# A two-layer transformer kernel: filler reordered, layer 2 begun early, softmax sums regathered by DMA

## The chip, the cores and the metric

One core of one Trainium2 chip. The metric is the device time of one execution in microseconds; lower is better. The time before is the median of three runs.

## The reference, cut to what matters

```python
x = A_x                                   # (1, 2048, 512) bf16
x = x + _A_ref(_layernorm(x), A_wqkv, A_wo)
x = x + _B_ref(_layernorm(x), B_w1, B_w2)
x = x + _A_ref(_layernorm(x), A_wqkv, A_wo)
x = x + _B_ref(_layernorm(x), B_w1, B_w2)
```

`_A_ref` is attention with 32 heads of 16 (softmax of q k / 4 over all 2048 keys, no mask, then the projection by `wo`); `_B_ref` is `relu(x @ w1) @ w2` with 1792 hidden columns. The normalization has neither gain nor bias, and both layers share their weights.

## The kernel before, in words

The 2048 rows are cut into 4 chunks of 512 (j), each of 4 row tiles of 128. Heads are handled in 8 units per chunk (t), 4 heads to a unit; two units (t = 2T and 2T + 1) share one 128-column stripe T of Q and K. There are 16 row blocks of keys (kb), 128 rows each. A unit is 16 row blocks x 4 heads = 64 blocks, and the main loop (`attention`, L411) takes 3 blocks per slot, so a unit is 21.3 slots, a chunk 170.7 and the kernel 1366.

In a slot TensorE computes three score blocks (L441) into one of two PSUM tiles `ps_s` of three banks, ScalarE takes the exponential of all three in one instruction (L448), and TensorE multiplies an earlier slot's exponentials by V (L389) into the one bank `ps_o`. V carries a column of ones, so the softmax sums come out as one row per head beside the head's 16 rows of output. At a unit's end VectorE copies `ps_o` (L366), spreads the sums by a shuffle (L369), takes reciprocals in four pieces (L372) and multiplies (L375), one of these per slot from `dve_q`.

All other matrix work is filler: after its attention part, each slot runs pieces of two matmuls from the queues `urgent` and `work`, in order and without looking whether the operands are there (`next_piece`, `run_some`); filler has one PSUM bank, `ps_f`. `urgent` holds the Q projection of the next unit. `work` holds, once a chunk's last unit is done, the rest of that chunk (`rest_of_chunk`, L337): 4 output projections of 8 matmuls, a layer normalization, 14 groups of 4 matmuls for the hidden layer, 4 groups of 14 for the second dense layer and, in layer 1, the next layer's normalization, K and V of that chunk. The evacuation of a group is issued right behind its last matmul. A normalization (`ln_groups`, `ln_stats`) issues statistics, the inverse root by four rounds of Newton and the apply on VectorE, and the transposes on TensorE in the same slot.

What a score or V block needs is forced out first (`run_until`). At the start that is K and V of each chunk in turn, as the first unit comes to them. At the end of each layer nothing is left to overlap with: the queues are run empty (L469 to L473) with all seven banks of `ps_s` and `ps_f` in rotation (`wide`). Layer 2's attention starts only behind that.

Q and the output projection use weights padded with zeros, `wq_pad` and `wo_pad`, made at the start by GpSimd and by 32 small DMAs, so that a unit's heads lie 32 rows apart.

## Time and profile before

| | |
|---|---|
| median of three runs | 2257.32 us (2256.94 to 2257.48) |
| the profiled execution, its own time | 2257.28 us |
| its span | 2255.5 us |
| TensorE busy, ScalarE busy | 1837.2 us, 1855.8 us |
| VectorE busy, GpSimd busy | 697.0 us, 12.6 us |
| mean granted TensorE clock | 0.723 of full |

The span runs from the first to the last instruction; the execution's own time is 1.8 us longer. Busy shares are means over the whole span, and the ends and the border between the layers are part of it. TensorE's clock is granted at one of two levels, so a mean of 0.723 is a mixture of stretches.

### The profile page before, as it was taken

What the parts mean: (1) busy time and instruction counts of PE and PEld (TensorE: products, weight loads), DVE (VectorE), ACT (ScalarE), POOL (GpSimd) and SP (SyncE); (2) the same over time, 40 slices, a digit from 0 to 9 for tenths busy, and PEclk for the clock granted to TensorE, in tenths of its full rate; (3) what the DMA queues carried; (4) which work ended last, traced back from release to release, by engine and by line L of the source; (5) the groups of instructions that cost most, each with busy time, mean ns of one, the idle gap of its engine ahead of it and who ended that gap; (6) DMA issues with size and microseconds to landing.
All of it is one profiled execution on the core that took longest, in us unless ns stands there. A gap on an engine that the chain in (4) does not pass through costs nothing.

```text
span 2255.5 us, 23128 instructions
## 1 busy us (share of the span) xinstructions
PE 1837.2 (81%) x10112; PEld 511.4 (23%) x10112; DVE 697.0 (31%) x1312; ACT 1855.8 (82%) x1367; POOL 12.6 (1%) x58
## 2 busy tenths in 40 slices
PE   4578887988878787988767888879887988878886
PEld 1122222222222222222222222222222222222222
DVE  5431124432253324332342122243114322142223
ACT  1279997989989898989505999989997999989970
POOL 2000000000000000000000000000000000000000
PEclk8775557986689757987576555689557975789558
DMA  4000000000000000000000000000000000000000
GB/s 140 0 1 1 1 0 1 1 1 1 1 1 1 1 1 1 1 1 1 1 0 1 1 1 1 1 1 10 1 1 1 3 8 1 1 1 10 1 1 10
DMA packets 9653, 11.44 MB, mean 5 GB/s; under 512 B 1104, under 2 KB 9040, under 8 KB 9552
## 3 DMA queue, kind: packets, MB, share of 16 engines
q1 hardware_dynamic: 8496, 8.92, 1.2%
q8 instruction: 79, 1.29, 0.2%
q10 hardware_dynamic: 1056, 1.05, 0.1%
q14 instruction: 22, 0.18, 0.0%
HBM read 7.86 MB, written 2.10 MB: 4 GB/s over the span
## 4 chain that ended last, share of the span: by engine, by line
ACT 62%; PE 25%; DVE 11%; issue 1%; POOL 0%; SPq 0%; DMA 0%; ACTq 0%; POOLq 0%; DVEq 0%
ACT e L448 62%; PE ps_f L263 8%; PE ps_s L441 6%; PE ps_o L389 5%; PE ps_s L263 4%; DVE stats L191 2%; DVE u L366 1%; PE ps_f L237 1%; DVE ht L319 1%; DVE r L372 1%; DVE vaug L291 1%; DVE xn L230 1%; DVE ktp L272 1%; DVE q L304 1%; DVE mv L192 0%
## 5 line engine op out<-in xcount | busy, mean ns | idle before, releaser
L448 ACT ACTIVATE e<-ps_s 128x1536 bf16<-128x1536 f32 (+1 forms) x1366 | 1854.5, 1551 | 298.6 <-PE ps_s L441 295.2
L441 PE MATMUL ps_s<-q,ktp 32*128 32x512 bf16 x4096 | 697.2, 497 | 168.7 <-ACT e L448 150.3
L389 PE MATMUL ps_o<-e,vaug 128*32 128x512 bf16 x4096 | 719.9, 506 | 33.9 <-DVE u L366 33.0
L441 PEld LDWEIGHTS <-ktp 32*128 32x128 bf16 x4096 | 215.8, 95 | 762.8 <-issue 744.4
L389 PEld LDWEIGHTS <-vaug 128*32 128x32 bf16 x4096 | 143.7, 97 | 492.9 <-issue 492.9
L372 DVE RECIPROCAL r<-r 128x128 f32<-128x128 f32 x256 | 221.9, 916 | 1.2
L304 DVE CAST q<-ps_f 128x512 bf16<-128x512 f32 x62 | 42.5, 685 | 501.3 <-PE ps_f L263 501.3
L366 DVE COPY u<-ps_o 128x512 f32<-128x512 f32 x64 | 44.2, 691 | 465.6 <-PE ps_o L389 465.0
L263 PE MATMUL ps_f<-xn2T,w 128*128 128x512 bf16 x352 | 110.8, 400 | 9.1 <-DVE q L304 0.8
L237 PE MATMUL ps_f<-ident,xn 128*128 128x128 bf16 x200 | 30.4, 307 | 103.1 <-DVE xn L230 103.1
L319 DVE TENSOR_SCALAR ht<-ps_f 128x512 bf16<-128x512 f32 x88 | 60.9, 692 | 148.1 <-PE ps_f L263 148.1
L263 PE MATMUL ps_f<-w,ht 128*128 128x512 bf16 x350 | 104.5, 383 | 0.8
L263 PE MATMUL ps_f<-xnT,wq_pad 128*128 128x512 bf16 x248 | 100.9, 499 | 5.1 <-DVE x L331 1.6
L263 PE MATMUL ps_f<-wo_pad,ot 128*128 128x512 bf16 x208 | 69.2, 422 | 4.1 <-DVE ot L375 2.6
L237 PEld LDWEIGHTS <-xn 128*128 128x128 bf16 x256 | 22.0, 130 | 174.5 <-DVE xn L230 174.5
L263 PEld LDWEIGHTS <-w 128*128 128x128 bf16 x448 | 37.7, 102 | 83.9 <-issue 70.5
L313 DVE TENSOR_TENSOR x<-x,ps_f 128x512 bf16<-128x512 bf16 x26 | 17.8, 685 | 113.7 <-PE ps_f L263 113.7
L237 PE MATMUL ps_s<-ident,xn 128*128 128x128 bf16 x56 | 8.5, 307 | 46.9 <-DVE xn L230 46.9
L369 DVE STREAM_SHUFFLE r<-u 128x512 f32<-128x512 f32 x64 | 46.2, 722 | 0.0
L331 DVE TENSOR_TENSOR x<-x,ps_f 128x512 bf16<-128x512 bf16 x25 | 17.1, 686 | 91.7 <-PE ps_f L263 91.7
L263 PEld LDWEIGHTS <-ht 128*128 128x128 bf16 x448 | 31.0, 97 | 60.5 <-issue 47.1
L375 DVE TENSOR_TENSOR ot<-u,r 128x512 bf16<-128x512 f32 x64 | 44.1, 689 | 1.6
(46 smaller groups left out, 459.7 us busy)
## 6 DMA issues: line engine op xcount, KB each, us to landing
w<-in_B_w_dram SPq DMA_DIRECT2D x2, 1792.0 KB, 9.7
x<-in_A_x_dram SPq DMA_DIRECT2D x16, 128.0 KB, 3.7
out_dram<-x SPq DMA_DIRECT2D x16, 128.0 KB, 1.7
wqkv<-in_A_wqkv_dram ACTq DMA_DIRECT2D x2, 512.0 KB, 5.3
wqkv<-in_A_wqkv_dram SPq DMA_DIRECT2D x1, 512.0 KB, 6.6
wo_pad<-in_A_wo_dram SPq DMA_DIRECT2D x32, 16.0 KB, 1.7
```

The lines of the kernel that those rows point to most:

```text
L191: nc.vector.bn_stats(out=st[:], in_=x_t[j * TPC + i][:])
L237: nc.tensor.transpose(pt[:, c * P : (c + 1) * P], xn[:, c * P : (c + 1) * P], ident[:])
L263: nc.tensor.matmul(b, lhsT, rhs, start=(i == 0), stop=(i == n - 1))
L304: nc.vector.tensor_copy(out=qbuf[n % 3][:], in_=b)
L319: nc.vector.tensor_scalar(out=ht[ft][:], in0=b, scalar1=0.0, scalar2=None, op0=ALU.max)
L366: nc.vector.tensor_copy(out=u[:], in_=ps_o[:])
L369: nc.vector.stream_shuffle(out=r[:], in_=u[:], mask=[lane] * 32)
L372: nc.vector.reciprocal(out=r[:, a : a + P], in_=r[:, a : a + P])
L375: nc.vector.tensor_mul(out=ot[t][:], in0=u[:], in1=r[:])
L389: nc.tensor.matmul(ps_o[32 * g : 32 * g + 32, :], vaug[l][kb][:, 4 * T + g, 2 * e : 2 * e + 32], slot["e"][:, w, :], start=(kb == 0), stop ...
L441: nc.tensor.matmul(b[:, w, :], kt[32 * g : 32 * g + 32, kc : kc + P], qbuf[n % 3][32 * g : 32 * g + 32, :], start=True, stop=True, tile_po ...
L448: ex = nc.scalar.activation(out=e[:, :m, :], in_=b[:, :m, :], func=ACTF.Exp, scale=SCALE)
```

## The change

- **Order of filler.** Each group carries the names of what it needs. A key is marked when its producer is issued (`mark`, some with a lag in slots), and a group is picked only if all its keys were marked in an earlier slot (`ready`, `pick`); other groups may overtake. Evacuations are queued in `evac` and issued behind the next slot's exponential. The parts of a normalization and of the softmax division are items of `dve_q` with costs, issued up to 900 ns a slot. `run_until` still forces (`force`) what a block needs. A slot runs at least one piece if one is ready.
- **Start.** Layer 1's four normalizations, K of the first pair and all of V are computed ahead of the first score, their PSUM evacuated by ScalarE (`nc.scalar.copy`). The other K groups become filler. The Newton rounds are three, not four.
- **Layer 2 begun early.** The first three pairs of layer 2's first chunk run on row blocks 0 to 11 and store their sums in `acc`; then the same three pairs run on blocks 12 to 15, and `acc` is added. K and V of chunk 4 are needed only by the second part.
- **Softmax sums.** Instead of the shuffle and four reciprocals, a DMA gathers the four rows of sums to 128 partitions x 16, VectorE takes one reciprocal, a DMA writes it back and a third spreads each row to 32 partitions. The very last unit keeps the shuffle, its reciprocal and multiply in quarters.
- **One Q projection per pair.** Q of a stripe is projected once and evacuated twice, each time multiplied by a 0/1 mask per row. The multiply at a unit's end applies the same mask, and `wo` is loaded unpadded by one DMA.

```diff
+    mask = [sb([P, 1], FP32, f"mask{e}") for e in range(2)]
     wqkv = sb([P, NDC, 3 * D], BF16, "wqkv")
-    wq_pad = [sb([P, NDC, P], BF16, f"wq_pad{t}") for t in range(NT)]
-    wo_pad = [sb([P, D], BF16, f"wo_pad{t}") for t in range(NT)]
+    wo = sb([P, NDC, D], BF16, "wo")
...
+    acc = [sb([P, QS], FP32, f"acc{t}") for t in range(NACC)]
     ebuf = [sb([P, W, QS], BF16, f"e{n}") for n in range(NE)]
-    qbuf = [sb([P, QS], BF16, f"q{n}") for n in range(3)]
+    qbuf = [[sb([P, QS], BF16, f"q{n}_{e}") for e in range(2)] for n in range(2)]
...
+    cbuf = [sb([P, QS // 32], FP32, f"c{n}") for n in range(2)]
...
+    warm = sb([P, 1], FP32, "warm")
...
-    nc.scalar.dma_start(out=wqkv[:, :, 0:D], in_=wq_src[:, :, 0:D])
-    nc.sync.dma_start(out=wqkv[:, :, D : 2 * D], in_=wq_src[:, :, D : 2 * D])
+    nc.scalar.dma_start(out=wqkv[:, :, D : 2 * D], in_=wq_src[:, :, D : 2 * D])
     nc.scalar.dma_start(out=wqkv[:, :, 2 * D : 3 * D], in_=wq_src[:, :, 2 * D : 3 * D])
     for tt in range(4, NTT):
         nc.sync.dma_start(out=x_t[tt][:], in_=x_flat[tt * P : (tt + 1) * P, :])
-
+    nc.scalar.dma_start(out=wqkv[:, :, 0:D], in_=wq_src[:, :, 0:D])
+    nc.sync.dma_start(out=wo[:], in_=A_wo[:, :].rearrange("(c p) f -> p c f", p=P))
+    nc.sync.dma_start(out=w1[:], in_=B_w1[:, :].rearrange("(c p) f -> p c f", p=P))
+    nc.sync.dma_start(out=w2[:], in_=B_w2[:, :].rearrange("(c p) f -> p c f", p=P))
+
+    nc.gpsimd.memset(warm[:], 0.0)
+    nc.scalar.activation(out=warm[:], in_=warm[:], func=ACTF.Exp)
...
-    for t in range(NT):
-        nc.gpsimd.memset(wq_pad[t][:], 0.0)
...
-    for t in range(NT):
-        T, e = divmod(t, 2)
-        nc.gpsimd.tensor_copy(
-            out=wq_pad[t][:].rearrange("p c (g e d) -> p c g e d", g=4, e=2)[:, :, :, e, :],
-            in_=wqkv[:, :, T * P : (T + 1) * P].rearrange(
-                "p c (g e d) -> p c g e d", g=4, e=2
-            )[:, :, :, e, :],
-        )
-    for t in range(NT):
-        nc.gpsimd.memset(wo_pad[t][:], 0.0)
-        T, e = divmod(t, 2)
...
-            nc.sync.dma_start(out=wo_pad[t][r0 : r0 + DH, :], in_=A_wo[DH * h : DH * h + DH, :])
...
+    def mark(key, lag=0):
+        made[key] = slot[0] + lag
...
+    def ready(deps):
+        return all(k in made and (wide[0] or made[k] < slot[0]) for k in deps)
...
+    evac = deque()
+    urgent = []
+    work = []
+    dve_q = []
...
+    def pick(test):
+        for q in (urgent, work):
+            for g in q:
+                if test(g["deps"]):
+                    q.remove(g)
+                    cur.extend(g["pieces"])
+                    return True
+        return False
+
+    def run_pe(budget):
         while budget > 0:
-            piece = next_piece()
-            if piece is None:
-                return
-            piece[1]()
-            budget -= piece[0]
+            if not cur:
+                if evac or not pick(ready):
+                    return
+            c, fn = cur.popleft()
+            fn()
+            budget -= c
...
+    def run_dve(budget):
+        i = 0
+        while i < len(dve_q) and budget > 0:
+            c, deps, fn = dve_q[i]
+            if ready(deps):
+                dve_q.pop(i)
+                fn()
+                budget -= c
...
+    def force():
+
+        if evac:
+            run_evac()
+            return True
+        if cur or pick(emitted):
+            cur.popleft()[1]()
+            return True
+        for i, (c, deps, fn) in enumerate(dve_q):
+            if emitted(deps):
+                dve_q.pop(i)
+                fn()
+                return True
+        return False
...
-        for _ in range(4):
...
-                    fin(b)
+                    evac.append(lambda: fin(b))
...
+        for _ in range(3):
...
+    def ln_rows(tag, j, i):
+
+        if tag not in ln_seq:
+            ln_seq.append(tag)
+        prev = ln_seq[ln_seq.index(tag) - 1]
+        dve_q.append((750, [], lambda: ln_stats(tag, j, i)))
+        if i == TPC - 1:
+            dve_q.append((2400, [], lambda: ln_rstd(tag)))
+            for k in range(TPC):
+                dve_q.append((420, [("xT", prev, k)], lambda k=k: ln_apply(tag, j, k)))
...
+    def ln_groups(tag, dst, war):
+        groups = []
+        for i in range(TPC):
+
+            def piece(i=i):
+                pt = ln_transpose(tag, i)
+
+                def fin():
+                    nc.vector.tensor_copy(out=dst[:, :, i * P : (i + 1) * P], in_=pt)
+                    mark(("xnT", tag, i))
+
+                evac.append(fin)
+
+            groups.append({"pieces": [(1.3, piece)], "deps": [("xn", tag, i)] + war})
...
+    def q_group(run, n, l, j, T):
+        def fin(b):
+            for e in range(2):
+                nc.vector.tensor_scalar(
+                    out=qbuf[n % 2][e][:], in0=b, scalar1=mask[e][:, 0:1], scalar2=None,
+                    op0=ALU.mult,
+                )
+            mark(("q", n))
 
         return mm_group(
-            [(wqkv[:, c, D + T * P : D + (T + 1) * P], xnT[j][:, c, :]) for c in range(NDC)], fin
-        )
...
-    def q_group(n, t, j):
-        def fin(b):
-            nc.vector.tensor_copy(out=qbuf[n % 3][:], in_=b)
-            done.add(("q", n))
-
-        return mm_group([(wq_pad[t][:, c, :], xnT[j][:, c, :]) for c in range(NDC)], fin)
...
+    def o_group(l, j, i):
         tt = j * TPC + i
 
         def fin(b):
             nc.vector.tensor_add(out=x_t[tt][:], in0=x_t[tt][:], in1=b)
-
-        return mm_group([(ot[t][:, i * P : (i + 1) * P], wo_pad[t][:]) for t in range(NT)], fin)
-
-    def h_group(ft):
+            mark(("o", l, j, i))
+            ln_rows(("ln2", l, j), j, i)
+
+        return mm_group(
+            [(ot[t][:, i * P : (i + 1) * P], wo[:, t // 2, :]) for t in range(NT)], fin,
+            [("ot", l, j, t, i) for t in range(NT)],
+        )
...
+            if wide[0] and ft % 2:
+                nc.scalar.activation(out=ht[ft][:], in_=b, func=ACTF.Relu)
+            else:
...
+            else:
+                ln_rows(("ln1", 1, j), j, i)
...
+            gs += ln_groups(("ln1", 1, j), xnT[j], [])
+            gs.append(k_group(1, 0, j))
+            gs += [v_group(1, kb) for kb in range(j * TPC, (j + 1) * TPC)]
+            gs += [k_group(1, T, j) for T in range(1, 4)]
...
+    segs = []
...
+    for j in range(NQS):
+        for T in range(4):
+            add_run(0, j, T, range(NKB), False, False)
+    early = range(NKB - TPC)
+    late = range(NKB - TPC, NKB)
+    for T in range(NACC // 2):
+        add_run(1, 0, T, early, False, True)
+    for T in range(NACC // 2):
+        add_run(1, 0, T, late, True, False)
+    for T in range(NACC // 2, 4):
+        add_run(1, 0, T, range(NKB), False, False)
+    for j in range(1, NQS):
+        for T in range(4):
+            add_run(1, j, T, range(NKB), False, False)
...
+        if sg["store"]:
+            nc.vector.tensor_copy(out=acc[t][:], in_=ps_o[:])
+            return
...
+        if sg["load"]:
+            nc.vector.tensor_add(out=u[:], in0=acc[t][:], in1=ps_o[:])
+        else:
+            nc.vector.tensor_copy(out=u[:], in_=ps_o[:])
...
+        def mul(a, w):
+            nc.vector.scalar_tensor_tensor(
+                out=ot[t][:, a : a + w], in0=u[:, a : a + w], scalar=mask[e][:, 0:1],
+                in1=r[:, a : a + w], op0=ALU.mult, op1=ALU.mult,
+            )
...
+        if last:
+            nc.vector.stream_shuffle(out=r[:], in_=u[:], mask=[lane] * 32)
+            for a in range(0, QS, P):
+                nc.vector.reciprocal(out=r[:, a : a + P], in_=r[:, a : a + P])
+                mul(a, P)
+        else:
+            sums = u[lane : P : 32, :]
+            nc.sync.dma_start(out=c[:], in_=sums)
+            mark(("c", n), 2)
+
+            def recip():
+                nc.vector.reciprocal(out=c[:], in_=c[:])
+                nc.sync.dma_start(out=sums, in_=c[:])
+                nc.sync.dma_start(
+                    out=r[:],
+                    in_=bass.AP(
+                        tensor=sums.tensor, offset=sums.offset,
+                        ap=[list(sums.ap[0]), [0, 32], [1, QS]],
+                    ),
+                )
+                mark(("r", n), 4)
+
+            dve_q.append((250, [("c", n)], recip))
+            dve_q.append((700, [("r", n)] + war, lambda: mul(0, QS)))
+        if t == NT - 1:
+            work.extend(rest_of_chunk(l, j))
...
+            if kb == sg["kbs"][-1] and g == 3:
+                finish_segment(sg, sg is segs[-1])
...
+    for j in range(NQS):
+        tag = ("ln1", 0, j)
+        for i in range(TPC):
+            ln_stats(tag, j, i)
+        ln_rstd(tag)
...
+        for i in range(TPC):
+            ln_apply(tag, j, i)
+            pt = ln_transpose(tag, i)
+            nc.scalar.copy(out=xnT[j][:, :, i * P : (i + 1) * P], in_=pt)
+            mark(("xnT", tag, i))
...
+        k_fin(0, 0, j, plain(k_mms(0, j)))
+        if j == 0:
+            urgent.append(q_group(None, 0, 0, 0, 0))
+            run_all()
+        for kb in range(j * TPC, (j + 1) * TPC):
+            nc.scalar.copy(out=v_out(0, kb), in_=v_in(plain(v_mms(kb))))
+            mark(("v", 0, kb))
+    for T in range(1, 4):
+        work.extend(k_group(0, T, j) for j in range(NQS))
...
+    blocks = deque((sg, kb, g) for sg in segs for kb in sg["kbs"] for g in range(4))
+    per_chunk = NT * NKB * 4 / W
+    wide[0] = False
...
+        for sg, kb, g in now:
+            if sg["n"] not in seen:
+                seen.add(sg["n"])
+                n = sg["n"] + 1
+                if n < len(runs):
+                    urgent.append(q_group(None, n, *runs[n]))
+            run_until(("q", sg["n"]))
+            run_until(("k", sg["l"], sg["T"], kb // TPC))
...
+        run_evac()
+        for sg, kb, g in now:
+            run_until(("v", sg["l"], kb))
...
-                dve_q.popleft()()
...
-            rest = len(blocks) / W % per_chunk
...
-            run_some(max(todo / max(rest - 6.0, 4.0), 0.01) if todo else 0)
-        drain_pv(0)
-        wide[0] = True
-        while dve_q:
-            dve_q.popleft()()
-        run_all()
...
+        pend.append({"e": eb, "blocks": deque(x + (w,) for w, x in enumerate(now))})
+        rest = len(blocks) / W % per_chunk
+        todo = left()
+        if todo:
+            run_pe(max(todo / max(rest - 12.0, 6.0), 1.0))
+        run_dve(900)
+    while pend:
+        emit_pv()
+    wide[0] = True
+    run_all()
...
```

## Rows read from the trace of the kernel before

**Rows 1.** The page: its parts 1 (busy us, share, instructions) and 4 (chain by engine).

```profile
PE 1837.2 (81%) x10112; PEld 511.4 (23%) x10112; DVE 697.0 (31%) x1312; ACT 1855.8 (82%) x1367; POOL 12.6 (1%) x58
...
ACT 62%; PE 25%; DVE 11%; issue 1%; POOL 0%; SPq 0%; DMA 0%; ACTq 0%; POOLq 0%; DVEq 0%
```

**Rows 2.** Groups by line and shape: count | busy us, mean ns | idle before us, releaser.

```profile
L448 ACT ACTIVATE e<-ps_s 128x1536 bf16<-128x1536 f32 x1364 | 1852.7, 1552 | 298.6 <-PE ps_s L441 295.2
...
L372 DVE RECIPROCAL r<-r 128x128 f32<-128x128 f32 x256 | 221.9, 916 | 1.2
...
L304 DVE CAST q<-ps_f 128x512 bf16<-128x512 f32 x62 | 42.5, 685 | 501.3 <-PE ps_f L263 501.3
```

**Rows 3.** ScalarE in order of time: start us, us, engine, line, operation, count [idle before].

```profile
37.97 4.13 ACT L448 ACTIVATE e<-ps_s 128x1536 bf16<-128x1536 f32 x3 [5.40 <-PE ps_s L441]
...
135.85 27.19 ACT L448 ACTIVATE e<-ps_s 128x1536 bf16<-128x1536 f32 x20 [0.66 <-PE ps_s L441]
...
386.17 1.45 ACT L448 ACTIVATE e<-ps_s 128x1536 bf16<-128x1536 f32 x1 [7.37 <-PE ps_s L441]
...
1205.55 31.18 ACT L448 ACTIVATE e<-ps_s 128x1536 bf16<-128x1536 f32 x23 [101.35 <-PE ps_s L441]
...
1983.52 1.45 ACT L448 ACTIVATE e<-ps_s 128x1536 bf16<-128x1536 f32 x1 [7.44 <-PE ps_s L441]
...
2160.49 25.20 ACT L448 ACTIVATE e<-ps_s 128x1536 bf16<-128x1536 f32 x19 [0.49 <-PE ps_s L441]
```

**Rows 4.** Busy us by stretch: PE, PEld, DVE, ACT, POOL; PE clock, DMA share, GB/s.

```profile
410.00:480.00 70.00, 62.01 (x398) 18.61 (x395) 29.06 (x46) 68.49 (x51) 0.00 (x0) 0.99 0.00 1
540.00:600.00 60.00, 52.88 (x269) 12.95 (x269) 11.89 (x19) 58.46 (x44) 0.00 (x0) 0.52 0.00 1
```

**Rows 5.** Order of time, all engines, 250 to 262 us: two filler pairs, neighbouring slots.

```profile
250.43 1.03 PE L263 MATMUL ps_f<-xnT,wq_pad 128*128 128x512 bf16 x2
...
252.49 0.74 PE L263 MATMUL ps_f<-xnT,wq_pad 128*128 128x512 bf16 x2
```

**Rows 6.** TensorE in order of time, 340 to 420 us, around a normalization.

```profile
384.97 0.61 PE L237 MATMUL ps_f<-ident,xn 128*128 128x128 bf16 x4 [7.56 <-DVE xn L230]
...
394.55 1.03 PE L263 MATMUL ps_f<-xn2T,w 128*128 128x512 bf16 x2
...
396.41 0.60 PE L263 MATMUL ps_f<-xn2T,w 128*128 128x512 bf16 x2
...
397.60 0.61 PE L263 MATMUL ps_f<-xn2T,w 128*128 128x512 bf16 x2
```

**Rows 7.** Order of time, all engines, 0 to 60 us.

```profile
8.16 0.66 DVE L191 BATCH_NORM_STATS2 stats<-x 128x6 f32<-128x512 bf16 x1
...
29.45 1.02 PE L263 MATMUL ps_s<-wqkv,xnT 128*128 128x512 bf16 x4 [0.78 <-DVE vaug L291]
...
39.97 0.68 DVE L191 BATCH_NORM_STATS2 stats<-x 128x6 f32<-128x512 bf16 x1
...
43.29 0.17 DVE L194 TENSOR_SCALAR va<-mv 128x4 f32<-128x4 f32 x1
...
46.26 0.41 DVE L230 TENSOR_SCALAR xn<-x,mv,ya 128x512 bf16<-128x512 bf16 x1
...
46.73 0.61 PE L237 MATMUL ps_f<-ident,xn 128*128 128x128 bf16 x4 [6.54 <-DVE xn L230]
...
47.37 0.42 DVE L240 COPY xnT<-ps_f 128x512 bf16<-128x512 bf16 x1 [0.70 <-PE ps_f L237]
```

**Rows 8.** The page: its parts 3 (packets, MB, share) and 6 (KB each, us to landing).

```profile
q1 hardware_dynamic: 8496, 8.92, 1.2%
...
wo_pad<-in_A_wo_dram SPq DMA_DIRECT2D x32, 16.0 KB, 1.7
```

**Rows 9.** Order of time, all engines, from 2180 us.

```profile
2186.39 0.69 DVE L366 COPY u<-ps_o 128x512 f32<-128x512 f32 x1 [22.25 <-PE ps_o L389]
...
2192.05 0.61 PE L263 MATMUL ps_s<-wo_pad,ot 128*128 128x512 bf16 x1 [3.18 <-DVE ot L375]
```

More of the change, by code (lines that the diff above doesn't have):

```diff
@@ L172, in run_until, with run_evac @@
+    def run_evac():
+        while evac:
+            evac.popleft()()
+    def force():
[11 more added lines that the diff above has]
+        return False
     def run_until(key):
-        while key not in done:
-            piece = next_piece()
-            assert piece is not None, key
-            piece[1]()
+        while key not in made:
+            assert force(), key
@@ L178, in run_all @@
     def run_all():
-        while True:
-            piece = next_piece()
-            if piece is None:
-                return
-            piece[1]()
-    def ln_stats(j):
-        n = ln_no[0] % 2
-        ln_no[0] += 1
-        for i in range(TPC):
-            st = stats[i % 2]
-            nc.vector.bn_stats(out=st[:], in_=x_t[j * TPC + i][:])
-            nc.vector.bn_aggr(out=mv[n][:, i, :], in_=st[:])
+        while force():
+            pass
+        assert not (urgent or work or dve_q or cur)
@@ new lines, in mm_group, with piece @@
+    def mm_group(mms, fin, deps, per=2):
+        hold = {}
+        pieces = []
+        n = len(mms)
+        for a in range(0, n, per):
+            def piece(a=a):
+                if a == 0:
+                    hold["b"] = bank()
+                b = hold["b"]
+                for i in range(a, min(a + per, n)):
+                    lhsT, rhs = mms[i]
+                    nc.tensor.matmul(b, lhsT, rhs, start=(i == 0), stop=(i == n - 1))
+                if a + per >= n:
+                    evac.append(lambda: fin(b))
+            pieces.append((min(per, n - a), piece))
+        return {"pieces": pieces, "deps": deps}
@@ L394, in emit_pv @@
                 tile_position=(0, 32 * g), skip_group_check=True,
             )
-            if kb == NKB - 1 and g == 3:
-                copy, rest = norm_items(n, t)
-                copy()
-                dve_q.extend(rest)
-                if t == NT - 1:
-                    dve_q.append(lambda l=l, j=j: work.extend(rest_of_chunk(l, j)))
-        if not slot["blocks"]:
-            pend.popleft()
-    def drain_pv(keep):
-        while len(pend) > keep:
-            emit_pv()
-    slot_no = 0
```

364 lines of the change are left out of this document (173 added, 191 removed).

## The prediction

> **What bounds the kernel now.** I began with the page's busy shares and its chain of waits [rows 1]: ScalarE is busy 82% of the span and TensorE 81%, and ScalarE carries 62% of the chain. So the exponentials set the pace. Grouped by line and shape, they are 1364 of one shape plus two short ones, 1852.7 us of busy time, hence 1.36 us each, and ScalarE sat idle 298.6 us before them, nearly all of it waiting for the score matmuls [rows 2]. The change leaves all 1366 exponentials as they are, so the question is what becomes of that idle time and of the two ends.
>
> ScalarE in order of time [rows 3] places it. The first exponential starts at 37.97. The 25th starts at 135.85, although 24 need 24 x 1.36 = 32.6 us: 65.3 us lost. At 386.17 there is a hole of 7.37; nine such (6.48 to 7.44, the last at 1983.52) hold 65.2 us together. At 1205.55 there is one of 101.35, the border between the layers. The last exponential ends at 2160.49 + 25.20 = 2185.7, 69.8 before the end of the span. Taking 5.4 (before the first), 65.3, 65.2 and 101.4 from 298.6 leaves 61 us of small holes. Check: 38 + 1853 + 293 + 69.8 = 2254, against a span of 2255.5. That profiled execution took 2257.28, 1.8 more than its span and within 0.1 of the median.
>
> The small holes: the granted clock is 0.99 of full while filler runs in every slot and 0.52 where attention runs alone [rows 4], that is mostly at 2.4 and at 1.2 GHz. In the slow state a slot with a filler pair lasts 252.49 - 250.43 = 2.06 us, 0.70 more than an exponential [rows 5]; in the fast one the same slot takes 397.60 - 396.41 = 1.19 [rows 6], and ScalarE is the limit again. So filler costs only where it starts from the slow clock: lone Q groups, and the first two pairs after a hole.
>
> **The change, part by part.**
>
> Start. Layer 1's four normalizations, K of the first pair and all V now come before the first score. Chunk 0: the fourth bn_stats and its aggregate end near 9.0 [rows 7]; the inverse root takes 43.29 to 46.26, fifteen small operations, and with one round of three fewer 2.4; two mask reductions have no row: between 0.2 (one small operation) and 0.42 (a copy), 0.25 each, as they read few elements; the first apply brings the first transpose to 12.4. A transpose-and-copy is 0.64 to the copy, plus the copy, now on ScalarE: no row has it; a third of an exponential, 0.45, is one end, the 0.69 of VectorE's cast [rows 2] the other, and 0.65 is taken, nearer the engine reading the same shape. The row at 29.45 waits 0.78 for an evacuation of another bank of the same PSUM tile [rows 7], so two of three transposes queue: four take 4.7, to 17.1. K 1.9, its cast 0.7, Q 1.9, two casts 1.4: VectorE is free at 23.0. Each further chunk is a chain through VectorE: statistics 3.3, root 2.4, apply 0.45, transposes 4.6, K 1.5 (1.0 to 1.9 by the clock), cast 0.7 = 13.0; three make 62. The last V groups add 6.5. First exponential at **69** (60 with copies of 0.45 and the fast clock; 80 if V delays each chunk's transposes). It comes 31 later than now, but the 65.3 behind it goes: 34 saved. The removed wq_pad and wo_pad work (32 DMAs, GpSimd copies) lies under this; the warm-up exponential's table load fits under the wait for x.
>
> Order of filler. I followed the new queue rule slot by slot, order only: one piece (two matmuls) per slot, about 690 slots with filler. A transpose is emitted only after its apply, so the nine 7.2 us holes go (TensorE waiting 7.56 for a normalization, [rows 6]). What is late next: the first transpose comes two slots after statistics (0.8), root (2.4) and applies were issued, some 4.3 us against about 3.3: 0.5 for each of 12 normalizations, 6 in all.
>
> Border. The first three pairs of layer 2 run on 12 of 16 row blocks: 6 units x 48 blocks / 3 = 96 slots. Chunk 4's remainder is 96 pieces, plus Q. Its first output projection is ready 11 slots in (gather lag, reciprocal, regather lag), the normalizations leave further holes, and the last piece of the second dense layer comes in the 94th slot. Then ten pieces are forced in a row: Q, four transposes, K, one V. From that last piece: add 0.7, statistics 0.8, root 2.4, three applies 1.2, Q casts 1.4, four transposes with copies at 1.1 and an apply 0.4, K 1.0 to 1.9, cast 0.75: 13 to 14 us, of which ScalarE covers about 4 with work in hand. Three more V groups force two pairs into a slot, 0.8 each or somewhat more. **14** instead of 101.4 (8 to 25). The six partial sums cost six copies and turn six copies into adds at 0.69, same place as now: nothing.
>
> Small holes. 35 Q groups for 64, but two casts at 0.69 each [rows 2] instead of one; about half of the 35 meet filler already running at the fast clock. Against that, filler now restarts from the slow clock after each normalization. I take 55 for 61 (35 if the lone Q's were most of it, 80 if each restart costs four pairs).
>
> Softmax sums. 63 units replace a shuffle and four reciprocals by a small reciprocal and three SP DMAs. VectorE (31% busy) gains nothing on the path. The added waits: the reciprocal is issued 3 slots after the copy, the multiply 5 slots, 6.7 us, after the reciprocal. An idle DMA lands in 1.7 [rows 8]; two with issue about 0.5 each and some transfer time, 5.7. In time, barely. Queued behind the waiting multiply on VectorE are the evacuations for which TensorE's filler waits; on SP, the next gather (16 slots off even in the short late units) and output stores, needed by nobody. I take 5 (0 to 23, below).
>
> Tail. The last unit keeps the shuffle, but multiplies in quarters right after each quarter's reciprocal. Of the 2192.05 - 2186.39 = 5.7 us between its copy and the rest of the output projection [rows 9], three reciprocals of 0.92 [rows 2] (some 2.5, as they overlap a little) and three quarters of the multiply leave the path: 2.9 saved; the root saves 0.6. The hidden layer stays held by the same-tile wait, whichever engine evacuates: nothing. **66.3** for 69.8.
>
> **Sum:** 69 + 1853 + (55 + 6 + 14 + 5) + 66.3 + 1.8 = **2070 us**.
>
> **Rivals.**
>
> Regather late. The regather reads four rows into 128. If four engines carry it, each moves 32 pieces; queue q1's 8496 packets at 1.2% of 16 x 2255.5 us are 51 ns each [rows 8], 0.1 for the 2 KB pieces: 3.3 to write back, 5.0 to spread, 1 of issue: 9.4, 2.7 after the multiply is due. Some 35 multiplies fall among filler; each would cost 2.7 + 0.7 less the slot and the buffer in hand, 0.65: 23 us, 2088. No row shows a four-row transfer, so I leave it at 0.2. The Trainium skill, "DMA: Bandwidth & Descriptors", section "Why a DMA increments its semaphore by 16 and not by 1", says that the engine count is the largest up to 16 dividing both sides' slowest dimension, which would make it four here and speaks for this rival.
>
> Border stays. If the chain leaves chunk 4 undone when its K is due, each piece not placed costs about 1.1; with nothing placed, 2070 + 87 = 2157. The counting speaks against it: 0.03.
>
> Fewer holes. Start at 61 and small holes of 35: 2042; 0.12.
>
> Slower: clock. Filler now has three or four holes per chunk, in which TensorE does attention alone; if filler then no longer lifts the clock, each of the 690 slots costs 0.70. From 187 / 0.70 = 267 such slots the gain is gone; half of them give 2070 + 240 = 2310. For it: after the 7.56 hole filler ran slow (1.03 for a pair). Against: two pairs later it ran at 0.60 [rows 6]. 0.05. The Trainium skill, "TensorE: Matmul & The Clock Gate", section "HAM oscillation", warns that bursts parted by waits each begin throttled; by that rule, the trace agrees for the two pairs, not for the rest.
>
> **How the numbers follow.** The forecast has 0.60, the rivals 0.20, 0.03, 0.12 and 0.05. The range takes in the first three likely ones with their bounds: start -9/+11, border -6/+11, small holes -20/+25, regather -5/+18, not all at one end at once: 2032 to 2110. 0.2% is 4.5 us, about what measurement tells from no change; only the clock case comes near or beyond the old time: 0.94 faster, 0.01 same, 0.05 slower.
>
> **What would show it.** First exponential near 69; no hole of 7 in ScalarE's rows inside a chunk; one of about 10 some 96 slots into layer 2; idle before the exponentials near 80; pairs of 0.60 through the dense layers; the multiply waiting little or nothing for DMA; last exponential about 66 before the end. Wrong if the multiply waits over 3 us, if dense pairs stay at 1.03, or if the border hole exceeds 25.

## The result, and the profile after

The changed kernel takes **2086.5 us** (2084.3 to 2092.3, four runs) against 2257.1 for the kernel before on the same chip: a ratio of 0.9248, 95% interval 0.9229 to 0.9267. The forecast was 2070 (2032 to 2110). It is faster, within the range and 16.5 us above the point; the rival "Regather late" gave 2088.

The page's busy shares and chain of waits of the changed kernel, which answer to [rows 1]:

```profile
PE 1752.3 (84%) x9873; PEld 490.5 (24%) x9996; DVE 437.0 (21%) x927; ACT 1876.7 (90%) x1407; POOL 2.4 (0%) x35
...
ACT 63%; PE 22%; DVE 9%; DMA 5%; issue 2%; SPq 0%; DVEq 0%
ACT e L616 62%; PE ps_f L236 7%; PE ps_s L609 6%; PE ps_o L538 5%; DMA r<-u 3%; DVE q L364 2%; PE ps_s L236 1%; DVE u L487 1%; PE ps_f L291 1%; DMA u<-c 1%; DVE ht L393 1%; PE ps_s L572 1%; DVE stats L253 1%; DVE ot L492 1%; DVE x L379 0%
```

ScalarE still carries the chain, now busy 90% of the span. New in the chain is DMA with 5%, of which `r<-u`, the transfer that spreads the reciprocals, has 3%.

The page's costliest groups of the changed kernel; the first answers to [rows 2], the second is the multiply at a unit's end:

```profile
L616 ACT ACTIVATE e<-ps_s 128x1536 bf16<-128x1536 f32 x1366 | 1852.9, 1563 | 97.9 <-PE ps_s L609 95.7
...
L492 DVE SCALAR_TENSOR_TENSOR ot<-u,mask,r 128x512 bf16<-128x512 f32 (+1 forms) x67 | 48.7, 727 | 342.1 <-DMA r<-u 337.9
```

The exponentials cost what they did (1852.9 us; before, 1854.5 for the same 1366), and the idle time before them fell from 298.6 to 97.9. VectorE stood 337.9 us in front of the multiply, waiting for that transfer: 56 times, 41 of them for more than 3 us.

ScalarE's timeline of the changed kernel at the first exponential, at the border and at the end, which answers to [rows 3] (columns: start, length, operation; in brackets the idle time before it):

```profile
68.77 6.83 ACT L616 ACTIVATE e<-ps_s 128x1536 bf16<-128x1536 f32 x5
...
1187.00 1.45 ACT L616 ACTIVATE e<-ps_s 128x1536 bf16<-128x1536 f32 x1 [10.28 <-PE ps_s L609]
1189.92 2.79 ACT L616 ACTIVATE e<-ps_s 128x1536 bf16<-128x1536 f32 x2 [1.47 <-PE ps_s L609]
1194.41 1.45 ACT L616 ACTIVATE e<-ps_s 128x1536 bf16<-128x1536 f32 x1 [1.70 <-PE ps_s L609]
1196.72 1.45 ACT L616 ACTIVATE e<-ps_s 128x1536 bf16<-128x1536 f32 x1 [0.85 <-PE ps_s L609]
1199.02 4.13 ACT L616 ACTIVATE e<-ps_s 128x1536 bf16<-128x1536 f32 x3 [0.85 <-PE ps_s L609]
...
1965.21 54.33 ACT L616 ACTIVATE e<-ps_s 128x1536 bf16<-128x1536 f32 x41 [0.48 <-PE ps_s L609]
```

The first exponential starts at 68.8, the last ends at 1965.21 + 54.33 = 2019.5, which is 65.8 before the end of the span of 2085.36. At the border five rows hold 10.28 + 1.47 + 1.70 + 0.85 + 0.85 = 15.2 us. No other hole of 7 us is left; the next longest has 2.98.

All engines of the changed kernel around one multiply, in order of time:

```profile
374.17 0.24 DVE L510 RECIPROCAL c<-c 128x16 f32<-128x16 f32 x1
374.44 0.55 SPq L511 DMA_DIRECT2D u<-c  x1
...
375.68 0.60 PE L236 MATMUL ps_f<-xn2T,w 128*128 128x512 bf16 x2
...
376.21 0.39 PE L609 MATMUL ps_s<-q,ktp 32*128 32x512 bf16 x3
376.23 0.53 SPq L512 DMA_DIRECT2D r<-u  x1
...
383.07 0.75 DVE L492 SCALAR_TENSOR_TENSOR ot<-u,mask,r 128x512 bf16<-128x512 f32 x1 [3.50 <-DMA r<-u]
383.74 0.68 DVE L393 TENSOR_SCALAR ht<-ps_f 128x512 bf16<-128x512 f32 x1
384.48 0.92 PE L236 MATMUL ps_f<-xn2T,w 128*128 128x512 bf16 x2 [2.42 <-DVE ht L393]
...
385.32 0.61 PE L609 MATMUL ps_s<-q,ktp 32*128 32x512 bf16 x3
...
385.98 1.45 ACT L616 ACTIVATE e<-ps_s 128x1536 bf16<-128x1536 f32 x1 [2.35 <-PE ps_s L609]
```

Read downwards, this is the mechanism in one place. The spread is issued at 376.23 and the multiply can start at 383.07, 6.8 us later. The multiply is at the head of VectorE's queue; behind it stands the evacuation of the hidden layer (L393), for which TensorE's next filler pair waits 2.42; the next scores stand behind that pair, and ScalarE loses 2.35. After the wait TensorE goes on at the lower of its two clocks: the three scores take 0.61, where they took 0.39 before it. The same trace in two stretches, where the third number from the end is the granted clock as a share of full (1.00 is 2.4 GHz; 0.53 is mostly 1.2):

```profile
376.00:382.00 6.00, 5.74 (x40) 1.61 (x39) 1.38 (x2) 6.00 (x5) 0.00 (x0) 1.00 0.20 42
...
384.40:388.00 3.60, 3.19 (x15) 0.63 (x15) 0.54 (x2) 1.45 (x1) 0.00 (x0) 0.53 0.00 0
```

In ScalarE's timeline I count 24 idle times over 0.3 us that stand within 6 us behind a multiply that waited for this transfer, 25.6 us together. Eight of them last 1.57 to 2.98 us and hold 16.6 of it, the others are under 1. So the idle time is made up of the border's 15.2, these 25.6 and 97.9 - 15.2 - 25.6 = 57.1 of small ones, some of the 25.6 being small ones that would stand there anyway.

Two of the eight stand where layer 2's first chunk is finished in short units:

```profile
1233.64 0.75 DVE L492 SCALAR_TENSOR_TENSOR ot<-u,mask,r 128x512 bf16<-128x512 f32 x1 [6.08 <-DMA r<-u]
1234.31 0.25 DVE L510 RECIPROCAL c<-c 128x16 f32<-128x16 f32 x1
...
1243.18 0.75 DVE L492 SCALAR_TENSOR_TENSOR ot<-u,mask,r 128x512 bf16<-128x512 f32 x1 [8.00 <-DMA r<-u]
...
1247.15 28.32 ACT L616 ACTIVATE e<-ps_s 128x1536 bf16<-128x1536 f32 x21 [2.98 <-PE ps_s L609]
```

A unit of four row blocks is 16 blocks, 5.3 slots or about 7.3 us. The multiplies follow 9.54 us apart, since each unit's reciprocal stands on VectorE behind the multiply of the unit before it. So the regathers line up there. In the run with the shuffle for the spread (below) the same two places have 0.49 and 0.91 instead of 1.57 and 2.98.

### The profile page after: what moved, and what is told of

Read it like the earlier page. It is cut to its first block, busy times and chain, and to the rows that moved or that the text cites. A ratio compares the mean times of both kernels' runs of the same rounds, so it can differ in the third digit from the quotient of the medians.

```text
span 2085.4 us, 22685 instructions
## 1 busy us (share of the span) xinstructions
PE 1752.3 (84%) x9873; PEld 490.5 (24%) x9996; DVE 437.0 (21%) x927; ACT 1876.7 (90%) x1407; POOL 2.4 (0%) x35
## 3 DMA queue, kind: packets, MB, share of 16 engines
q10 hardware_dynamic: 1584, 1.57, 0.2%
## 4 chain that ended last, share of the span: by engine, by line
ACT 63%; PE 22%; DVE 9%; DMA 5%; issue 2%; SPq 0%; DVEq 0%
ACT e L616 62%; PE ps_f L236 7%; PE ps_s L609 6%; PE ps_o L538 5%; DMA r<-u 3%; DVE q L364 2%; PE ps_s L236 1%; DVE u L487 1%; PE ps_f L291 1%; DMA u<-c 1%; DVE ht L393 1%; PE ps_s L572 1%; DVE stats L253 1%; DVE ot L492 1%; DVE x L379 0%
## 5 line engine op out<-in xcount | busy, mean ns | idle before, releaser
L616 ACT ACTIVATE e<-ps_s 128x1536 bf16<-128x1536 f32 x1366 | 1852.9, 1563 | 97.9 <-PE ps_s L609 95.7
L236 PE MATMUL ps_f<-xn2T,w 128*128 128x512 bf16 x366 | 117.6, 397 | 18.8 <-DVE ht L393 5.1
L236 PE MATMUL ps_f<-w,ht 128*128 128x512 bf16 x377 | 117.4, 389 | 10.0 <-DVE q L364 4.9
L492 DVE SCALAR_TENSOR_TENSOR ot<-u,mask,r 128x512 bf16<-128x512 f32 (+1 forms) x67 | 48.7, 727 | 342.1 <-DMA r<-u 337.9
L487 DVE COPY u<-ps_o 128x512 f32<-128x512 f32 x58 | 39.9, 689 | 356.0 <-PE ps_o L538 355.5
L393 DVE TENSOR_SCALAR ht<-ps_f 128x512 bf16<-128x512 f32 x99 | 68.4, 691 | 197.1 <-PE ps_f L236 197.0
L236 PE MATMUL ps_f<-xnT,wqkv 128*128 128x512 bf16 x218 | 82.1, 452 | 14.0 <-DVE ktp L331 5.4
L364 DVE TENSOR_SCALAR q<-ps_f,mask 128x512 bf16<-128x512 f32 x68 | 47.8, 744 | 197.5 <-PE ps_f L236 188.6
L236 PE MATMUL ps_f<-wo,ot 128*128 128x512 bf16 x203 | 69.6, 419 | 5.3 <-issue 3.6
L253 DVE BATCH_NORM_STATS2 stats<-x 128x6 f32<-128x512 bf16 x64 | 43.8, 684 | 7.0 <-DMA x<-in_A_x_dram 5.8
L331 DVE CAST ktp<-ps_f 128x512 bf16<-128x512 f32 x28 | 19.3, 690 | 53.7 <-PE ps_f L236 53.7
```

What stands on the lines that cost most here:

```text
L236: nc.tensor.matmul(b, lhsT, rhs, start=(i == 0), stop=(i == n - 1))
L253: nc.vector.bn_stats(out=st[:], in_=x_t[j * TPC + i][:])
L364: nc.vector.tensor_scalar(out=qbuf[n % 2][e][:], in0=b, scalar1=mask[e][:, 0:1], scalar2=None, op0=ALU.mult,)
L393: nc.vector.tensor_scalar(out=ht[ft][:], in0=b, scalar1=0.0, scalar2=None, op0=ALU.max)
L487: nc.vector.tensor_copy(out=u[:], in_=ps_o[:])
L492: nc.vector.scalar_tensor_tensor(out=ot[t][:, a : a + w], in0=u[:, a : a + w], scalar=mask[e][:, 0:1], in1=r[:, a : a + w], op0=ALU.mult, ...
```

## The experiments

A first set of four, on the changed kernel (before: 2256.8 us in that set).

**Shuffle for the spread.** The gather, the reciprocal and the writing back stay; the third transfer goes, and VectorE's shuffle spreads the row.

```diff
-                nc.sync.dma_start(
-                    out=r[:],
...
+            def spread():
+                nc.vector.stream_shuffle(out=r[:], in_=u[:], mask=[lane] * 32)
+                mul(0, QS)
...
```

> The changed kernel with the third DMA of the softmax division (each row of reciprocals to 32 partitions) replaced by VectorE's shuffle, issued with the multiply in the same slot as before; the first two DMAs stay. Theory A (the regather is late: the multiply waits 338 us in all for the third DMA, and the evacuations behind it hold up filler): these waits vanish, the ScalarE holes that follow a multiply (some 20 us of the 98) vanish, 2067 us. Theory B (the holes come from filler restarting at the slow clock, the wait is idle time of an idle engine): 2085 to 2090 us. The shuffle's 0.72 us a unit on VectorE is on no path in either.

Measured: 2070.0 us (2066.2 to 2073.3), ratio 0.9170 [0.9157, 0.9182]: 16.5 below the changed kernel.

**Multiply later.** All three transfers stay, the multiply is due four slots later, with a third set of buffers.

```diff
...
-                mark(("r", n), 4)
+                mark(("r", n), 8)
```

> The changed kernel with its three DMAs, but the multiply issued four slots later (lag 8 for 4), with three buffers each for sums, reciprocals and gathered sums instead of two. Theory A: VectorE waits no more, the holes behind multiplies go as in the run with the shuffle, but every chunk's filler starts four slots later and at the border about four more pieces are forced: 2067 + 4 = 2071 us. Theory B: 2087 to 2093 us. A third view, that the spread DMA disturbs other accesses while it moves data, would leave the time near 2087 here and lower it with the shuffle.

Measured: 2069.9 us (2069.8 to 2077.5), ratio 0.9182 [0.9168, 0.9196]. The two groups of its page:

```profile
L616 ACT ACTIVATE e<-ps_s 128x1536 bf16<-128x1536 f32 x1366 | 1852.1, 1568 | 82.7 <-PE ps_s L609 80.0
...
L492 DVE SCALAR_TENSOR_TENSOR ot<-u,mask,r 128x512 bf16<-128x512 f32 (+1 forms) x67 | 48.4, 722 | 268.3 <-DMA r<-u 268.1
```

The same transfers move the same bytes, and the same 16.6 us are gone: it was the multiply's place ahead of the evacuations, not the transfers' traffic. The third set of buffers was not run by itself; in the changed kernel, though, VectorE's copy of a unit's output stands 356.0 us idle, 355.5 of them for TensorE, so the profile shows no wait for a buffer there. The row of the multiply shows too how little such a sum of waits says: 268.1 us are left, where VectorE has nothing else to do, and the time is that of the run with the shuffle, where the multiply has 2.4.

**Four head pairs early.** Layer 2 is begun on four pairs, not three.

```diff
-    NACC = 6
+    NACC = 8
```

> The changed kernel with all four pairs of layer 2's first chunk begun on 12 row blocks (eight partial sums for six): 128 slots, not 96, before the last K and V of layer 2 are needed. Theory (the border's 15 us are pieces forced because chunk 4's filler needs about 104 slots): nothing is forced any more, the hole of 10.3 and the four behind it vanish, two more short units cost under 2 us: 2087 - 13 = 2074 us. Rival (the border hole is the dependency chain of the normalization itself): it moves but stays, 2085 to 2089 us.

Measured: 2078.6 us (2069.6 to 2081.4), ratio 0.9201 [0.9182, 0.9221]. The longest idle time of ScalarE after its start is 3.02 us: the border's 10.28 is gone. Its idle time before the exponentials is 86.6 for 97.9, so 11 us less where the medians differ by 8.

**Shuffle and four reciprocals for all units**, as in the kernel before.

```diff
-            sums = u[lane : P : 32, :]
-            nc.sync.dma_start(out=c[:], in_=sums)
...
+            dve_q.append((700, [], shuf))
+            for a in range(0, QS, P):
+                dve_q.append((900, [("s", n)], lambda a=a: recip(a)))
...
```

> The changed kernel with the softmax division as in the kernel before: shuffle, four reciprocals, multiply, one item per slot, no DMA. Theory A (the DMA detour brought only waits): as with the shuffle for the third DMA, 2067 us, or 2 us more, since 0.92 us reciprocals sit ahead of evacuations; filler of a chunk starts about as early. Theory B: 2085 to 2090. If the reciprocals on VectorE were what the change removed from the path, 2095 or more.

Measured: 2064.2 us (2062.5 to 2065.3), ratio 0.9144 [0.9131, 0.9156]. The regather by DMA costs this kernel 22 us: it took VectorE from 33% busy to 21%, and VectorE was not what the exponentials waited for. The late spread is 16.5 of them; the other 5.8 lie between this run and the one that keeps the gather and the writing back, and no run shows what in these two costs that. The runs also lie closer together without it (2.8 us between the ends, not 8.0). This kernel is the base of the next set of four (before: 2257.4 us in that set).

**No early start of layer 2.**

```diff
-    NACC = 6
+    NACC = 0
```

> Written on the version with the shuffle for all units (2064.22 us): layer 2 starts with whole units, no partial sums. Theory: the hole at the layers' border is hidden by the early row blocks and by nothing else. Without them the last chunk's out-projection, norms, FFN and K projection stand between two exps again, as in the kernel before with its 101.35 us: +70 to +110, so 2135 to 2175 us, and one idle time of ScalarE of 80 to 120 us. Rival: the order of the filler alone closes most of it; then the longest idle time is under 40 us and the run under 2100 us.

Measured: 2137.3 us (2136.1 to 2137.6), 73 above its base. ScalarE's timeline at the border:

```profile
1134.49 1.45 ACT L610 ACTIVATE e<-ps_s 128x1536 bf16<-128x1536 f32 x1 [85.34 <-PE ps_s L603]
```

So it is the early row blocks that hide the border: with the order of the filler in place and without them, 85.3 of the 101.4 us stay.

**Order of filler off.** A group no longer waits a slot for its operands: the first one in the list whose operands have been issued goes, and where there is none, the next item of a normalization is issued at once. The evacuations, too, go out at once instead of behind the next exponential, so the run takes these rules together.

```diff
-                if evac or not pick(ready):
-                    return
+                run_evac()
+                if not pick(emitted):
+                    for i, (c, deps, fn) in enumerate(dve_q):
+                        if c in (750, 2400, 420) and emitted(deps):
+                            dve_q.pop(i)
+                            fn()
+                            break
...
```

> Written on the version with the shuffle for all units (2064.22 us): filler groups are taken strictly in the order of the list again, and the work of a normalization is given out where its transposes stand, so that TensorE meets them with VectorE's chain still to run. Theory: each of the 11 normalizations inside the attention stretch (8 but the one in the tail, and 4 between layers) costs a hole on ScalarE of 4 to 7.5 us again, +45 to +75, so 2110 to 2140 us. Rival (the exps' own buffering hides most of it now): 11 holes of under 2 us, 2064 to 2080 us.

Measured: 2092.1 us (2090.8 to 2095.7), 28 above its base: holes come back, with lengths between those of the theory and the rival. One of them, in all engines' timeline of that run:

```profile
338.13 0.69 DVE L261 BATCH_NORM_STATS2 stats<-x 128x6 f32<-128x512 bf16 x1
338.86 0.18 DVE L262 BATCH_NORM_AGGREGATE mv<-stats 128x2 f32<-128x6 f32 x1
339.07 0.17 DVE L267 TENSOR_SCALAR va<-mv 128x4 f32<-128x4 f32 x1
...
341.46 0.41 DVE L289 TENSOR_SCALAR xn<-x,mv,ya 128x512 bf16<-128x512 bf16 x1
...
341.93 0.61 PE L299 MATMUL ps_f<-ident,xn 128*128 128x128 bf16 x4 [4.56 <-DVE xn L289]
...
343.12 1.45 ACT L618 ACTIVATE e<-ps_s 128x1536 bf16<-128x1536 f32 x1 [3.84 <-PE ps_s L611]
```

Where [rows 6] had TensorE wait 7.56, it waits 4.56 here: the first three row tiles' statistics went out with their rows, so that one tile's (0.69 + 0.18), the root (2.4, one round of Newton shorter) and one apply (0.41) are left. Twelve holes of 2.8 to 3.9 make 41 us, eleven at a normalization and one at pieces forced at the border; the base's border hole of 9.0 is not among them, so 32 of it are new. So the order is worth 28 us on top of the statistics' new place and the shorter root, and together they remove the nine 7-us holes of before. What the statistics' place and the root are worth is read from these rows; no run takes them by themselves.

**One Q projection per unit.**

```diff
...
-                n = sg["n"] + 1
+                n, e = (sg["n"], 1) if sg["e"] == 0 else (sg["n"] + 1, 0)
                 if n < len(runs):
-                    urgent.append(q_group(None, n, *runs[n]))
+                    urgent.append(q_group(e, n, *runs[n]))
...
```

> Written on the version with the shuffle for all units (2064.22 us): one Q projection for each unit (one cast each) in place of one for each pair (two casts), so some 35 groups of four matmuls more, 60 us of TensorE at 0.43 us each, and as many casts as before. Theory: where attention runs alone there is room under the exps, where filler stands dense there is not: about half of it is seen, or less, since filler moves into the room: +5 to +25, so 2070 to 2090 us. Rival (all hidden): 2062 to 2067 us.

Measured: 2073.4 us (2073.0 to 2073.8), 9 above its base. 140 matmuls more (10136 for 9996) of about 0.46 us are 65 us of TensorE, of which one seventh is seen; 4.7 of it at the border, whose hole has 13.67 instead of 8.96. TensorE's busy time itself grew by only 18 us (1768.1 to 1786.4): the mean granted clock went from 0.741 to 0.762, and the scores' 4096 matmuls took 674.2 us instead of 688.4. So a part of the added work was made up by the other matmuls, which ran at the higher clock for longer.

**Banks in turn.** In the start and the tail, where seven PSUM banks go round, the six of `ps_s` are taken from its two tiles alternately.

```diff
-        return ps_s[n // W][:, n % W, :]
+        return ps_s[n % 2][:, n // 2, :]
```

> Written on the version with the shuffle for all units (2064.22 us): only in the start and the tail, the six banks that the attention tiles lend are taken from the two tiles in turn, not three of one tile and then three of the other. Theory: a write into one bank waits for the read of another bank of the same tile (0.78 us in the start's rows), so the start loses 1 to 3 us and the tail 3 to 8: 2054 to 2061 us. Rival (the waits are for the evictions themselves): 2062 to 2067 us.

Measured: 2042.3 us (2039.9 to 2043.9), ratio 0.9044 [0.9029, 0.9059]: 22 below its base, twice the most that I had expected. The changed kernel's V projections of the first chunk:

```profile
23.85 0.58 ACT L580 CAST vaug<-ps_s 128x512 bf16<-128x512 f32 x1 [0.28 <-PE ps_s L572]
24.48 1.02 PE L572 MATMUL ps_s<-wqkv,xnT 128*128 128x512 bf16 x4 [0.67 <-ACT vaug L580]
25.55 0.58 ACT L580 CAST vaug<-ps_s 128x512 bf16<-128x512 f32 x1 [1.11 <-PE ps_s L572]
```

and the same with the banks in turn:

```profile
19.93 2.75 PE L566 MATMUL ps_s<-wqkv,xnT 128*128 128x512 bf16 x12
...
21.00 0.58 ACT L574 CAST vaug<-ps_s 128x512 bf16<-128x512 f32 x1 [0.28 <-PE ps_s L566]
21.86 0.58 ACT L574 CAST vaug<-ps_s 128x512 bf16<-128x512 f32 x1 [0.28 <-PE ps_s L566]
22.72 0.58 ACT L574 CAST vaug<-ps_s 128x512 bf16<-128x512 f32 x1 [0.28 <-PE ps_s L566]
```

Before, a matmul into one bank waited for the copy out of another bank of the same tile, and the two engines took turns, 1.7 us a group. Now three groups stand in one row without a wait and the copies follow 0.86 apart. The first exponential comes at 60.2 instead of 68.5 in the base, the tail shrinks from 66.6 to 54.3.

This is the base of the last set (before: 2257.0 us in that set), but for the third kernel.

**Hold at a unit's end.** In the slot in which a unit ends, the next unit's first products with V are left to the next slot (`done[0]` counts the units that have ended).

```diff
...
         while len(pend) > 1:
+            ended = done[0]
             emit_pv()
+            if done[0] != ended:
+                break
```

> Written on the version with the shuffle and the banks in turn (2042.29 us): in the slot in which a unit ends, the next unit's first probabilities-times-V products are held back to the next slot, so that TensorE has the next scores to run while VectorE copies the unit out of its only bank. Theory: of ScalarE's 64 us of small idle times there, 25.6 us in 41 stand behind a wait of TensorE for that copy, and most of this goes: 2020 to 2032 us. Rival (the held products crowd the next slot, and the idle time moves there): 2038 to 2046 us.

Measured: 2010.9 us (2009.6 to 2013.2), ratio 0.8909 [0.8896, 0.8922]: 31 below its base and 9 below the expected range. The products with V by form, in the base and then in this run:

```profile
L532 PE MATMUL ps_o<-e,vaug 128*32 128x512 bf16 x4096 | 713.6, 500 | 44.5 <-DVE u L487 35.0 <-DVE acc L478 5.0 <-DVE u L485 4.3
```

```profile
L534 PE MATMUL ps_o<-e,vaug 128*32 128x512 bf16 x4096 | 686.8, 492 | 9.0 <-DVE u L489 7.4 <-DVE u L487 1.4 <-ACT e L612 0.2
```

TensorE's wait for the copy out of its one output bank falls from 44.5 to 9.0 us, and ScalarE's idle time before the exponentials from 76.2 to 48.3. The held products did not crowd the next slot.

**Statistics ahead in the start.**

```diff
...
+        if j + 1 < NQS:
+            for i in range(TPC):
+                ln_stats(("ln1", 0, j + 1), j + 1, i)
+            ln_rstd(("ln1", 0, j + 1))
         k_fin(0, 0, j, plain(k_mms(0, j)))
```

> Written on the version with the shuffle and the banks in turn (2042.29 us): in the start the next row chunk's statistics and reciprocal roots stand ahead of this chunk's K cast on VectorE. Theory: the start is now VectorE's chain, 11.3 us a chunk (K, cast, four statistics, root, normalize, transposes), and TensorE's part of it goes out of it, about 3 us for each of three chunks: 2031 to 2036 us, first exp 8 to 10 us sooner. Rival (TensorE or ScalarE bounds the start as soon as the chain gives way): 2039 to 2043 us.

Measured: 2030.2 us (2029.5 to 2030.8), ratio 0.8993 [0.8980, 0.9007], 12 below its base and just below the expected range; the first exponential comes at 46.84 instead of 60.21. So in the base VectorE's chain, not TensorE, set the start.

**The spread in four transfers**, on the changed kernel itself.

```diff
-                    out=r[:],
...
+                for g in range(4):
+                    row = u[32 * g + lane : 32 * g + lane + 1, :]
+                    nc.sync.dma_start(
+                        out=r[32 * g : 32 * g + 32, :],
...
+                            ap=[list(row.ap[0]), [0, 32], [1, QS]],
```

> Written on the changed kernel itself (2086.51 us): the transfer that spreads the reciprocals is issued as four, one for each source row of 2 KB read 32 times. Theory (a transfer's packets are dealt out by source row, so one row is one DMA engine's work): 32 packets of 156 ns still stand in one row, and three issues more come with it: the multiply still waits, 2083 to 2093 us. Rival (each of the four is dealt out over all engines, some 1.5 us in place of 5.2): the multiply no longer waits, and the time falls to that of the shuffle, 2064 to 2072 us.

Measured: 2135.0 us (2134.0 to 2136.7), ratio 0.9458 [0.9444, 0.9473]: 48 slower than the changed kernel, which neither view expected. The DMA view from 360 to 400 us, one digit a microsecond in tenths of 16 engines, of the changed kernel and then of this run:

```profile
DMA  0000000000000000013222100000000000000000
...
DMA packets 397, 0.29 MB, mean 7 GB/s; under 512 B 268, under 2 KB 268, under 8 KB 396
...
q1 hardware_dynamic: 396, 0.28, 3.5%
```

```profile
DMA  0000000000000000000789858210000000000000
...
DMA packets 457, 0.30 MB, mean 7 GB/s; under 512 B 328, under 2 KB 328, under 8 KB 456
...
q1 hardware_dynamic: 456, 0.28, 13.5%
```

One transfer kept two tenths of the 16 engines busy in most of these digits, that is some four (2 stands for 3.2 to 4.8); the four transfers keep five to nine tenths busy and more. So they were dealt out over far more than four engines, against my theory, and it did not help, against the rival: all packets of the stretch took 13.5% x 16 x 40 = 86 us in place of 22. Nearly all of that is the same 128 pieces of 2 KB, 0.16 us each in the packet records of the changed kernel and 0.65 in those of this run. With one row read by many engines at once each piece takes four times as long. Whether the shared row does it or only the number of engines at work, no run separates. Three more issues come on top. Multiplies wait longer, here 9.2 us from the first issue to the multiply (378.03 to 387.19) instead of 6.8:

```profile
378.03 3.20 SPq L514 DMA_DIRECT2D r<-u  x4
...
387.19 0.75 DVE L492 SCALAR_TENSOR_TENSOR ot<-u,mask,r 128x512 bf16<-128x512 f32 x1 [6.06 <-DMA r<-u]
```

**Together.** Shuffle, four pairs, banks in turn, statistics ahead, hold, and VectorE's items first where the queues are run empty.

```diff
-    NACC = 6
+    NACC = 8
...
+        for i, (c, deps, fn) in enumerate(dve_q):
+            if emitted(deps):
...
         if cur or pick(emitted):
...
```

> Together, on the version with the shuffle and the banks in turn (2042.29 us): layer 2 begun on four head pairs in place of three, the statistics ahead in the start, the products held back at a unit's end, and VectorE's items first where the queues are run empty. Theory: the terms add: -10 for the border, -9 for the start, -16 for the units' ends: 2007 us, 1995 to 2020. Rival (they share the same idle times): 2020 to 2035 us.

Measured: **1988.3 us** (1986.9 to 1989.1), ratio 0.8809 [0.8794, 0.8824], 98 below the changed kernel. Its page:

```profile
PE 1694.7 (85%) x9874; PEld 494.7 (25%) x10000; DVE 681.6 (34%) x1246; ACT 1870.8 (94%) x1407; POOL 2.4 (0%) x35
...
L616 ACT ACTIVATE e<-ps_s 128x1536 bf16<-128x1536 f32 x1366 | 1847.6, 1643 | 39.7 <-PE ps_s L609 37.0
```

46.9 until the first exponential, 1847.6 + 39.7 of attention and 51.4 after the last make 1985.6 (span 1985.1; the 0.5 before the first exponential is counted twice). The longest idle time is 0.91 us. The terms added, and the hold (31 for 16) and the start (12 for 9) were each larger than I took them, which is why the sum lies 19 below its forecast and below its range. VectorE's items first was not run by itself. What is left to win beside the exponentials is the start, the tail and 40 us.

## Why the prediction was right, and where it was off

- **Bound.** Right: the exponentials are still the floor (1852.9), and the question was the idle time and the ends.
- **Start.** Forecast 69, measured 68.8. VectorE's chain was named as the limit; the run with the statistics ahead shows it for the version with the banks in turn. In the changed kernel the same-tile wait held the start too: without it the first exponential comes 8 us sooner. ScalarE's copy takes 0.59 (0.65 taken), and the copies queue by that wait as forecast.
- **Order of filler.** Right in what goes: no 7-us hole is left inside a chunk. But the prediction put all 65.2 us down to the order, and the run without it loses 28; by the rows the rest belongs to the statistics that go out with each row tile and to the shorter root.
- **Clock.** Dense pairs take 0.60 (the row at 375.68 and four more up to 380.80, at a granted clock of 1.00), so the slower rival's condition did not come. The mean granted clock is 0.736, after 0.723.
- **Border.** Forecast 14 (8 to 25), measured 15.2, and the hole of 10.28 stands 96 slots into layer 2, as said; without the early blocks 85.3 in one hole, with a fourth pair none. The terms written down make about 12 (13 to 14, less 4, and three times 0.8), and 14 takes them up; measured were 10.28 and 4.9.
- **Small holes.** 55 + 6 taken for other idle time, 57 measured. One Q projection per pair gives 9 us. The run with the hold shows what nearly half of these small holes were: TensorE waiting for the one output bank at a unit's end, 28 us of ScalarE's idle time. That had no term in the prediction, which put the time down to the slow clock [rows 4], so that its number fits here is luck. The page of before had the wait:

```profile
L389 PE MATMUL ps_o<-e,vaug 128*32 128x512 bf16 x4096 | 719.9, 506 | 33.9 <-DVE u L366 33.0
```

- **Tail.** Forecast 66.3, measured 65.8. "The hidden layer stays held by the same-tile wait" held, and the run with the banks in turn shows that this wait was worth 12 us there.
- **Softmax sums: the step that failed.** The prediction said "two with issue about 0.5 each and some transfer time, 5.7. In time, barely", and took 5 us. Measured from the reciprocal's end to the multiply: 383.07 - 374.41 = 8.7 us. The writing back was quick (1.8, where the rival had 3.3), the spread slow (6.8, where it had 5.5 with its issue). The rows behind the 5.7 were loads of 16 KB from memory [rows 8]; a transfer out of four rows was not among them, and its pieces take 0.16 us where 51 ns per packet had made 0.1. The queue behind the waiting multiply on VectorE, and who would wait for it, were named rightly. Wrong was "the next gather (16 slots off even in the short late units)": 16 slots are the early units, which gather nothing, and the late ones are 5.3, so that there the regathers line up, with holes of 1.57 and 2.98. So the **rival "Regather late"** happened, at 22 us by the shuffle for all units and 17 by the later multiply, priced at 23 and given a chance of 0.2. The sign set for it, "Wrong if the multiply waits over 3 us", came 41 times. But it was badly chosen: with the later multiply such waits still come 31 times and cost nothing. The Trainium skill, "DMA: Bandwidth & Descriptors", section "Why a DMA increments its semaphore by 16 and not by 1", makes it four engines for four source rows and sixteen for one row read 32 times. The DMA view agrees with the four (some four busy) and is in line with the sixteen (up to nine tenths busy, so 14 or more), and this rule should have weighed more than the mean of a queue. What the packets cost with more engines on the same row was in no row of before.

With the regather at 22 instead of 5 the sum is 2087, and 2086.5 was measured (idle before the exponentials 97.9, where "near 80" was named). That it fits so well is in part luck: the small holes had another cause than the one in the sum, and the rival's 23 was 35 multiplies at 0.65, where the trace has eight idle times of 1.57 to 2.98 us and sixteen under 1.

## What to carry to other kernels

Work moved off an engine that was not the bound gained nothing here, and as what replaced it was waited for at the head of a queue, everything behind it paid: before shortening such a transfer, compare the time until the consumer's slot with the slowest transfer, or move the consumer later. A sum of waits in front of one instruction says little until one has followed one case to the engine that sets the pace. And when a bound engine loses half a microsecond at regular places, look for a buffer that exists only once: here one output bank and banks that share a tile cost 31 and 22 us, each mended by a few lines.

## What the runs showed that was not expected

- Pieces of 64 bytes were cheap (the writing back, 128 of them, takes 1.8 us from issue to the next issue). 128 pieces of 2 KB were not: 0.16 us each from four rows in one transfer, 0.65 with the four rows in transfers of their own.
- Where TensorE waits less, the exponentials themselves ran a little shorter: 1847.3 us in all with the hold, 1851.9 in its base. Why was not tried.
